# Two thirds of the w_out conversion beside the first layer instead of the attention, with a new order table, another queue for one pair and fewer warm-up products

## The chip, the cores and the metric

One core of one Trainium2 chip. The metric is the device time of one execution in microseconds, lower is better; the figure for the kernel before is the median of three runs. The engines of the core run side by side, each its own instructions in order: TensorE (PE, matrix products; PEld are its weight loads), VectorE (DVE), ScalarE (ACT), GpSimd (POOL) and SyncE (SP). SP, ACT and POOL also issue transfers (DMA) between the chip's memory (DRAM) and the core's, each on a queue of its own. Products come out in PSUM, which has 8 banks.

## The reference, cut to what matters

```python
def _attn_ref(q, k, v):                       # batch 4, 12 heads, 448 positions, 64 wide
    scores = scale * np.matmul(q, k.transpose(0, 1, 3, 2)) - np.log(S)
    attn = 1.0 / (1.0 + np.exp(-scores))      # a sigmoid, not a softmax
    return np.matmul(attn, v).astype(np.float32)

def _moe_ref(x, w_gate, w_val, w_out, rms_g): # 1792 tokens, 768 wide, 1536 inside
    rms = np.sqrt(np.mean(x * x, axis=-1, keepdims=True) + 1e-06)
    xn = x / rms * rms_g
    g = xn @ w_gate
    silu = g * (1.0 / (1.0 + np.exp(-g)))
    val = xn @ w_val
    return (silu * val @ w_out).astype(np.float32)

def _moe2_ref(x, w_in, w_out):                # 2048 inside
    h = x @ w_in
    g = h - np.tanh(h)
    return (g @ w_out).astype(np.float32)
```

The output is `_moe2_ref(_moe_ref(_attn_ref(q, k, v)))`, the heads laid side by side. q, k and v come in 32-bit floats, the weights of both layers in 64-bit floats.

## The kernel before

**Stages.** First the attention, two heads (a pair) at a time, 6 pairs for each of the 4 batches. Then the first layer: products with w_gate and w_val (called Ag and Av; phase A) and with w_out (phase B). Then the second: w_in (C) and w_out2 (D). Each layer is done for batches 0 and 1 first (BATCHES[0]), then for 2 and 3.

**Products.** A 32-bit factor is split into a high and a low part that TensorE multiplies fast, and three products (high-high, high-low, low-high) stand for one. On top of that, matrices are taken as 2 by 2 blocks and multiplied with seven block products instead of eight, from sums such as S1 to S4 of the weights' blocks A11 to A22 and T1 to T4 of the activations'. So for each weight VectorE and ACT make values, sums and parts. `values32` (L510) makes a 32-bit value out of a raw 64-bit tile `raw`: a cast into the tile `zero` (by ACT or VectorE, L438 in the profile, the line of a helper) and one VectorE instruction at L510. `total` (L574) makes a sum. `split` (L521) makes the two parts. There are 2 buffers for `raw`, one tile `zero` for all, and at most 3 buffers `cv` for values and sums.

**Jobs.** The first layer's first half is a list of jobs 0 to 14: five pair jobs (Ag, Av, Ag, Av, Ag; 21 products of three each), a job of phase B with set 0 of w_out (42 of three), four pair jobs, set 1, three pair jobs, set 2 (used plain, with the four blocks alone). Each job makes the factors of the job two ahead (`conv`) and loads the raw tiles of the one four ahead (`load`).

**w_out.** Its blocks come in three sets. `rows_early` makes a set's units: load the raw tiles by POOL's queue, convert, sum, and store the values in DRAM, again by POOL, as `wB`. Set 0 and 1 have four blocks and, less one, the four sums, 7 stores; set 2 has four stores. Jobs 5, 10 and 14 load them again. In the kernel before all three sets' units, with casts by VectorE (`by_dve`), are spread over the attention of batches 0 to 2 (`rows_b`, `ROWS_B`). The second layer's w_out2 (D), four sets, goes the same way beside the first layer's second half.

**q, k and v.** `pair_load` loads a pair: q and k by SP's queue, but 128 columns of the very first k by ACT's, v of batches 0 and 1 by POOL's. From the third pair on q and k are split as well (`split_qk`, L732).

**The order.** The code adds each piece of work with its reads, writes and buffers to a plan; `lay` then gives it out. Among the pieces that can start soon it takes the one of lowest rank in `ORDER`, a table of one number for every piece, written out as text. So the order of instructions on each engine, and with it the order of the queues, is the table's, within what the buffers' caps allow. The program issues them with semaphores, and an engine that waits holds all behind it.

**Warm-up.** `N_WARM` products of zeros (L446) run on TensorE while the first q and k come in.

Of the kernel before, what the change touches and what calls it, by code (L numbers as in the profile page):

```python
# [244 lines left out]
2zn2ZU5fM7Lu9LSBC672y4ss0WM24q3fM0n70DR5fq0IM1G233P3oh48l3l61M_1do2Cr89Q96_0uM16r2S522A3HH1yx3Ou3Pf29E2f34LM2Do37L2k52Cr
2_y3fn48I3B61Oe4Pg2xM0kg3iv4fn3h42Gn14W3CM2cp3Zw3wM45d41K4BD4AF4QI2GK2u62h_1wT41k4J61gB2g94vR4vM1J43Tf3sS4aY1-l56T1-M12j
3hI0dw1Hx1pZ2FZ3ky3gy2Iy1oi1rH2tX1JA5912Mt2lT2r13G80xf02v3Z_37B0S43IB1rE0R32vN5Ae49D4p-3BP6184MVNGI5NB3hZ8ZS1ri1M94P_2i0
2o_33O3sX32b29L18k1Py1Kf3Vz2Ux2PE3he0_l3Bv2OB2u81l034i2o92Xj3P22Au2AU2mq1n91uv07m0mV2Gx1Rx24y2pH0zp1cc0QE2m63lw1KL33Y0n1
2J34dY2x22fg11V14E2845Lx12n3mr3RK3D35PL3Wv4qC4Oy6DU2hU5KQ4-92Sc3Fh0tO4Db3uN1Va4SY3fT3Sz2uz3e51Ox1nS3Na2nW5M37oH2_Y3ky2Lz
2YU35b1vK3u83FE2B22l33Nz63u4ZS56n3lO2hT4S_5gk3-d5P25IR5U943P0i45TW5r97OX5Eh3Pq3XA2YK5dv0gg4et2pX7pi0QV4Gz3ek4Cs3IC2Hu5b9  # L250
4zu5KT4TC4Rp1Ry1oL4nH37734N3fh2iy4nD3oi5tk3dh4Ob7aV4a44wb0X-73K0473l464X3hg3lA4Hj2gY3TT3j93fe2rb7dP4l95fy4pU5gu33g49S5Hg
4PC7fg3Ro44b58A02W5iV5mg4_R50j3x64aH4SI6qg38b5nU49DAG44OU3yV6RP7Ab6iJBwR5mz12p2nm4rH39r4HS5fq96I4W84FD76r1390Xa3Qk0Rh03Q
8Do42w5HrH4y7MZ43J4HF6qn39p47i5wJ4FF87_3x72cc2s50Jr0D43130s70m-1JE4Gs0GWH1V7MD3DbEyb2lE4ke7eg73Q8aF77IE0202-4OO6zz7y05Eu
0h06ME63l54u4IZ6PTBAv02-5vZ71w4wlAxB9GX38kABw9my0GY7lA7Wr3NZ3rF9tN3SF7pO69PAUP5A05ZG2ll3oQ57F4ay2rw8WQ2wW0001PkAIr3870kT
5LC5CIDOS0Wt0Yo4p368E6ni0VC5kA9vd4QIIY_0NQJwm0TM7UBAb2EalG2n64g51w6yp5WV6ip6bp6T8A8s3ed1qF4ma2IU1157Cc4Rz1C28W0BeP7-y6as
8Tw5h76W-0M04gw7YO8cECVP6XW8pN5BH7pk2G92bJ6kc7Le7aM0aD1O0A898DQ0go7dABk444L0wU5r18O83xP5Qr0J63tfDjl1pD81HByz7PQ3349qK6Sk
1R9BtyE6UB18CdFFuMDtH0cO9NY6wv19EBL13i4IHv6bJBJOElH8tX76e9M9DSfBxmGch6Rw5BDBxw3zh1y5BsU7Yp7g67gJ2a002-EMV7TM3If4xG7a800r
9YI1wL9oC5pP04TKFB5iGB4a0PA8ie0VD0d0FecAJrBY79pfFdDCAo5h4B10DHp0BuHbOK3y9UjAVxCFo5NDD48EwUNPHD1YFcsHhpDBrIZmERY16X0TQGN8
EyvD-qE3A6Lt0Z90EDGcwDV50YV0Dv0BtEVBEDe9EZ0CKGn3Cta4ao0pSCvq0D_000LGuAdI9nZ81WAcC8n62nUElp38pATI7bqM2DA0h8Nj6B3FVE1asPdV
6oUGOW4djEOZPqvNZ1NKMHyoC6TC-xBEfCLs9Dp7ZABW794g4QuDKjDCBCoMCIuBn0ARDBh0DnmFRa87x2a41OI1QC05f05gKLoEqWHotGQe6BsINu8t_8PI  # L260
MT70XMMx28aV6gGAyFKpwDkE43O1_85ko220McH1DM1ug6ncKj997d5X87gOJjf0WfOcA8L_7xmATvLur79b96QNQ2PHt0aPHSEOq9UikIxMIahJAnPM9LlP
AuNJ7ZEeLIMCFABJQvGFxEhr9vp6uZ6-bFoq7m38FgDIn9AN6zi7gzE7o7ih7Qv7GM6br5Z08Ei63qEND6ts7Q55NO9vn5lu6Aj9C791L6Pa7a36sk6vY8UU
6z05uz9OT8-NCSFBmn1Cn7xz6ua6aG7bM5u87NI7FA4fC7TD9rT82Q6pn4xg7-AARL3NTAE46Fn7cs8aJ6Yy6xm6hd8R29PU6-S8L257u5sb6Fa7Kf7AM6bE
5E55K08DM6Z_5jR8aD3Lo7oo67U6iG6ZE6bh7LA6Zc6zP7vi6Rn5pf7ew7aZ6rc83E7PC76p7JF8nN6Gw8z97rO78w4_s6li6GJ6FY63U59Y5DP2YH3Jy2_g
8xY61w6Vy3Cg6x-5ti5Pt49L68C7iL6Hw4Ch6zW7YM7Au4zQ3TT4TH3oQ8WP5Tw7k73Lm7M26Zl6yH7sW7AH5sk5Tk7kA7io7lb7Ra7035RW9pA8f40G02oX
6bM7fl8tW6dd79571T6oe7oc8B_7MH5E157B3uS4_x9OL4_o3sR7gE69w7kH8dX75U7Ol53N2y_3bH6dd6AA2P872_5Ek8076oX3NO6mG5_q55g7s16Fa61n
5fb8Aa81_7xB7Au87C3-T6jj7tQ7oL2z59g883U8Yv3Do7qO7a79Bm74l9022gT8MW8Sh51R1Lv5mp7yV7bW73a7AZ7w86Zl9RX4aq4lh5Jh8SG9So6V075V
87f8q65wD7_08Fs6yJ8Dc8ZUA0W7jq8Dk75-7Iy8QZ75Z7n18628SI8oS8EF6rI4pr76X88G6NU7b56-V4hm8Rn7628QD8THBps8y492Y6yX7lr7wv8yC6g2
6jO8IaAAe8QW7gz7SbAJV5pQ97u7d_9e_8ce7nk5sQ6eC8U77Qs87O8ry8b16oN7O58dB6bO7Lj73F7UP85s8eR7eTAAQ8pK7O87r79DT7xc90tAIQ87SA-v
# [1125 lines left out]
```

## Time and profile before

| | us |
|---|---|
| median of 3 runs (1032.61 to 1040.37) | 1033.85 |
| the profiled execution | 1032.65 |
| its span, first to last instruction | 1030.8 |
| TensorE busy | 1015.3 (98%) |
| VectorE busy | 790.4 (77%) |
| ACT busy | 676.7 (66%) |
| POOL busy | 155.8 (15%) |

Busy times overlap, and a busy TensorE need not be at its pace, since its products are pipelined and their ends modelled: how many it sends in a stretch tells more. Times in rows are us from the span's start. The attention is from the start to about 140 us, the first layer's first half from there to about 380 us, its second half to about 620 us, the second layer from there to the end.

### The profile page before, as it was taken

The page shows a single profiled execution, that of the slowest core. Times are in us where ns is not written, and L with a number is a line of the kernel's source. Part 1 is how long each engine was busy: PE and PEld are TensorE (multiplying, and loading weights), DVE is VectorE, ACT ScalarE, POOL GpSimd, SP SyncE. Part 2 cuts the span into 40 slices and gives each one's busy share as a digit, 9 for nine tenths or more (in the row PEclk, how much of TensorE's full clock was granted, in tenths as well). Part 3 has the DMA queues.
Part 4 walks back from the last instruction along what each step waited for, and adds up shares of the span by engine and source line. Part 5 has one row for each costly group of instructions (what it writes and reads, how often), then busy time and mean ns, then how long its engine had stood idle before and what let it go on. Part 6 is the DMA issues. An engine that isn't in the chain of part 4 may idle for free.

```text
span 1030.8 us, 15321 instructions
## 1 busy us (share of the span) xinstructions
PE 1015.3 (98%) x5261; PEld 876.4 (85%) x5261; DVE 790.4 (77%) x1281; ACT 676.7 (66%) x1235; POOL 155.8 (15%) x217
## 2 busy tenths in 40 slices
...
GB/s 312 285 338 309 234 235 235 298 189 305 197 195 327 141 259 319 361 265 355 214 128 242 219 199 266 99 311 254 235 159 252 264 188 94 225 129 197 121 228 135
DMA packets 101997, 240.03 MB, mean 233 GB/s; under 512 B 11456, under 2 KB 59520, under 8 KB 101920
## 3 DMA queue, kind: packets, MB, share of 16 engines
...
q8 instruction: 41, 0.67, 0.3%
...
HBM read 149.36 MB, written 89.66 MB: 232 GB/s over the span
## 4 chain that ended last, share of the span: by engine, by line
PE 69%; issue 13%; DMA 10%; DVE 3%; POOL 3%; ACT 1%; SPq 0%; POOLq 0%; DVEq 0%; ACTq 0%
PE ps L1135 37%; PE ps L1080 21%; PE ps L1160 6%; PE ps L813 3%; DMA part<-in_qkt 2%; DMA wD<-part 2%; PE ps L756 2%; POOL out L958 2%; DMA out<-unit 1%; DMA part<-wAg 1%; DMA part<-wB 1%; DMA raw<-in_w_out 1%; DMA wB<-part 1%; DVE part L521 1%; PE ps L777 0%
## 5 line engine op out<-in xcount | busy, mean ns | idle before, releaser
L1135 PE MATMUL ps<-unit,part 128*128 128x448 f32 x2520 | 521.0, 365 | 8.4 <-DVE unit L1016 4.6
L1135 PEld LDWEIGHTS ps<-unit,part 128*128 128x128 f32 x2520 | 470.9, 187 | 52.4 <-DVE unit L1016 6.3
L1080 PE MATMUL ps<-unit,part 128*128 128x448 f32 x1512 | 311.4, 364 | 0.0
L1080 PEld LDWEIGHTS ps<-unit,part 128*128 128x128 f32 x1512 | 283.5, 187 | 22.3
L521 DVE TENSOR_TENSOR part<-part 128x768 fp32r<-128x768 f32 (+1 forms) x244 | 215.4, 891 | 76.8 <-ACT part L438 55.0
L438 ACT COPY unit<-ps 128x448 f32<-128x448 f32 x291 | 150.3, 536 | 127.1 <-PE ps L1135 46.5
L438 ACT CAST part<-part 128x768 fp32r<-128x768 f32 (+1 forms) x236 | 183.1, 786 | 41.1 <-DMA wD<-part 8.0
L887 DVE TENSOR_TENSOR unit<-unit 128x448 fp32r<-128x448 f32 x252 | 152.1, 620 | 35.2 <-ACT unit L438 27.1
L438 ACT CAST unit<-unit 128x448 fp32r<-128x448 f32 x262 | 143.3, 570 | 39.3 <-DVE unit L999 17.9
L1016 DVE TENSOR_TENSOR unit<-ps,unit 128x448 f32<-128x448 f32 x168 | 103.9, 622 | 48.0 <-PE ps L1135 19.1
L765 ACT ACTIVATE unit<-ps 128x448 f32<-128x448 f32 x168 | 80.3, 565 | 27.6 <-PE ps L756 15.3
L892 DVE TENSOR_TENSOR unit<-unit 128x448 f32<-128x448 f32 x144 | 86.4, 619 | 14.4 <-DMA unit<-sumB 7.9
L958 POOL DMA_DIRECT2D sumB<-unit x48 | 41.8, 946 | 273.2 <-DVE unit L1016 168.8
L510 DVE SCALAR_TENSOR_TENSOR part<-raw,zero 128x768 uint32<-128x768 uint32 x68 | 64.8, 953 | 6.4 <-ACT zero L438 5.9
L438 ACT CAST zero<-raw 128x768 f16<-128x768 bf16 x52 | 56.0, 1078 | 16.5 <-DMA raw<-in_w_out 6.5
L813 PE MATMUL ps<-unit,part 128*64 128x448 f32 x288 | 59.4, 548 | 0.0
L1160 PE MATMUL ps<-unit,part 128*128 128x448 f32 x288 | 59.2, 364 | 0.0
L958 POOL DMA_DIRECT2D out<-unit x36 | 31.1, 1055 | 175.3 <-DVE unit L1016 161.7
L1160 PEld LDWEIGHTS ps<-unit,part 128*128 128x128 f32 x288 | 54.0, 187 | 4.2
L756 PEld LDWEIGHTS ps<-unit 64*128 64x128 f32 x396 | 35.6, 184 | 17.7 <-ACT unit L765 9.8
L756 PE MATMUL ps<-unit 64*128 64x448 f32 x396 | 47.3, 375 | 0.5 <-DVE unit L732 0.5
L813 PEld LDWEIGHTS ps<-unit,part 128*64 128x64 f32 x288 | 18.5, 136 | 30.5 <-issue 23.8
...
## 6 DMA issues: line engine op xcount, KB each, us to landing
raw<-in_w_out POOLq DMA_DIRECT2D x28, 768.0 KB, 7.9
part<-wD SPq DMA_DIRECT2D x56, 384.0 KB, 6.8
part<-wB SPq DMA_DIRECT2D x36, 384.0 KB, 5.5
raw<-in_w_in SPq DMA_DIRECT2D x16, 768.0 KB, 5.1
wC<-part SPq DMA_DIRECT2D x30, 384.0 KB, 3.3
part<-wC SPq DMA_DIRECT2D x30, 384.0 KB, 3.9
...
wD<-part POOLq DMA_DIRECT2D x28, 384.0 KB, 7.0
```

What stands on the lines that cost most here:

```text
L438: add(engines, lambda e: (nc.scalar.copy if e == "ACT" else nc.vector.tensor_copy)(to(), of()), reads, writes)
L521: add({**dve(n, psum=False), **pool(n)}, lambda e: ENG[e].tensor_sub(lo(), of(), hi().bitcast(F32)), [*reads, *kh], [*kl])
L756: nc.tensor.matmul(ps[i].tile[:, :S], lhsT=k_of(w, b, c, i), rhs=x.tile[rows, :S], start=q == 0, stop=q == len(terms) - 1)
L765: add(act(S, psum=True), lambda e: nc.scalar.activation(to.tile, ps.tile[:, :S], AF.Sigmoid, bias=-math.log(S), scale=1.0 / math.sqrt(D)), ...
L813: nc.tensor.matmul(ps.tile[HEADS[i], :S], lhsT=v_of(v, b, c, i), rhs=a[c][i].tile, start=opens and c == 0, stop=not opens and c == MAIN - ...
L887: add({**pool(S), **dve(S, psum=False)}, lambda e: ENG[e].tensor_sub(t["l"].tile, of.tile, t["h"].tile.bitcast(F32)), [of["t"], kh], [kl])
L892: add({**dve(S, psum=False), **pool(S)}, lambda e: ENG[e].tensor_sub(t.tile, x.tile, y.tile), [x["t"], y["t"]], [t["t"]])
L958: add(queue("POOL", True), lambda e: nc.gpsimd.dma_start(out=d.tile, in_=t.tile, accum_op=ALU.add), [t["t"], d["t"]], [d["t"]], moved=move ...
L1016: add(dve(S), lambda e: nc.vector.tensor_add(t.tile, ps.tile[:, :S], t.tile), [ps["t"], t["t"]], [t["t"]])
L1080: nc.tensor.matmul(ps.tile[:, :S], lhsT=part(a), rhs=x[b].tile, start=n in (1, 5) and kp == 0 and q == 0, stop=kp == n_kp - 1 and q == 2, ...
L1135: nc.tensor.matmul(ps.tile[:, :S], lhsT=part(a), rhs=x[b].tile, start=n in ((1, 2, 5) if opening else (1, 5)) and i == 0 and q == 0, stop= ...
L1160: nc.tensor.matmul(ps.tile[:, :S], lhsT=wt, rhs=a[p].tile, start=start and i == 0, stop=stop and i == 2, skip_group_check=True)
```

## The change

Five things. `N_WARM` goes from 9 to 7. The cap of `cv` goes from 3 to 5 buffers, in the same room of 20. q and k of the second pair (batch 0, pair 1) are issued by ACT instead of SP. The units of sets 1 and 2 of w_out are no longer in `rows_b`; they are added beside the first layer's jobs 2, 3, 4 (set 1) and 6, 7, 8 (set 2), where ACT makes the casts. And every number of the table `ORDER` is new, so that all engines' order is new.

```diff
-N_WARM = 9
+N_WARM = 7
+ROWS_AT = {1: 2, 2: 6}
...
-        "part": (N_PART, {"cv": 3, "again": 4, "vs": 6, "qkr": 9, "whl": 8, "op": 10}),
+        "part": (N_PART, {"cv": 5, "again": 4, "vs": 6, "qkr": 9, "whl": 8, "op": 10}),
...
-        part("SP", lambda: tq.tile, both[:, :S], tq[0], 4 * S)
+        first = "ACT" if (b, p) == (0, 1) else "SP"
+        part(first, lambda: tq.tile, both[:, :S], tq[0], 4 * S)
...
-            part("ACT" if hi == P else "SP", lambda lo=lo, hi=hi: tk.tile[:, lo:hi], both[:, S + lo:S + hi], tk[n], 4 * (hi - lo))
+            part("ACT" if hi == P else first, lambda lo=lo, hi=hi: tk.tile[:, lo:hi], both[:, S + lo:S + hi], tk[n], 4 * (hi - lo))
...
-    rows_b = by_dve([u for i in range(n_sets("B")) for u in rows_early("B", i)])
+    rows_b = by_dve([u for i in range(n_sets("B") - len(ROWS_AT)) for u in rows_early("B", i)])
...
+    rows_late = {}
+    for i, at in ROWS_AT.items():
+        rows = rows_early("B", i)
+        rows_late.update({at: rows[:1], at + 1: rows[1:5], at + 2: rows[5:]})
...
-        ahead = conv(j + AHEAD) + [lambda: load(j + 2 * AHEAD)]
+        ahead = conv(j + AHEAD) + rows_late.get(j, []) + [lambda: load(j + 2 * AHEAD)]
```

What the table makes of it, at three places. Lines of the changed kernel are one or two higher: L438 is L439 there, L510 is L511, L732 is L734, L756 is L758, L777 is L779, L797 is L799, L813 is L815, L849 is L851.

VectorE at the opening, the kernel before from its fourth instruction on (`part` is q or k, `unit` a part of it, `raw` a tile of w_out):

```order
L438 CAST unit<-part 128x448
L732 TENSOR_TENSOR unit<-part,unit 128x448
L438 CAST zero<-raw 128x768
L438 CAST unit<-part 128x384
L510 SCALAR_TENSOR_TENSOR part<-raw,zero 128x768
L732 TENSOR_TENSOR unit<-part,unit 128x384
```

The same place of the changed kernel:

```order
L439 CAST unit<-part 128x448
L734 TENSOR_TENSOR unit<-part,unit 128x448
L734 TENSOR_TENSOR unit<-part,unit 128x384
L439 CAST unit<-part 128x448
L734 TENSOR_TENSOR unit<-part,unit 128x448
L439 CAST unit<-part 128x384
```

The raw tile of w_out has gone from between the splits of the third pair, and POOL's loads of w_out stand behind the v of six pairs.

TensorE around the norm of batch 1 (L849), the kernel before (L756 are scores, L777 and L797 the pairs' last positions, L813 products with v):

```order
L797 MATMUL ps<-unit,part 64x448 x4
L756 MATMUL ps<-unit 128x448 x18
L813 MATMUL ps<-unit,part 64x448 x6
L756 MATMUL ps<-unit 128x448 x18
L813 MATMUL ps<-unit,part 64x448 x6
L777 MATMUL ps<-part 64x448 x4
L797 MATMUL ps<-unit,part 64x448 x4
L849 MATMUL ps<-ones,unit 128x1 x3
```

The same of the changed kernel, from the same L799 on:

```order
L799 MATMUL ps<-unit,part 64x448 x4
L758 MATMUL ps<-unit 128x448 x18
L815 MATMUL ps<-unit,part 64x448 x6
L758 MATMUL ps<-unit 128x448 x12
L851 MATMUL ps<-ones,unit 128x1 x3
```

The norm has moved forward by 6 products of scores, 6 of v and the tail.

ACT beside job 8 of the first layer, the kernel before (with buffer numbers; `raw_3455` is a tile of w_gate):

```order
L438 CAST part_3521<-part_3496 128x768
L438 CAST zero_80<-raw_3455 128x768
L438 COPY unit_3540<-ps_3478 128x448
L438 COPY unit_3548<-ps_3485 128x448
L438 COPY unit_3554<-ps_3492 128x448
```

The changed kernel (`raw_3218`, `raw_3298` and `raw_3349` are tiles of w_out):

```order
L439 CAST zero_80<-raw_3218 128x768
L439 CAST part_3325<-part_3161 128x768
L439 COPY ps_3335<-ps_3310 128x448
L439 CAST part_3342<-part_3205 128x384
L439 CAST zero_80<-raw_3298 128x768
L439 COPY unit_3365<-ps_3345 128x448
L439 CAST part_3371<-part_3148 128x768
L439 COPY unit_3386<-ps_3310 128x448
L998 ACTIVATE unit_3401<-ps_3335 128x448
L439 CAST unit_3408<-unit_2831 128x448
L439 CAST zero_80<-raw_3349 128x768
```

Three casts of w_out tiles now stand among the copies out of PSUM (`ps`) of this job.

## Rows read from the trace of the kernel before

**Rows 1.** The page, part 1: TensorE's busy time, share of the span, instructions
```profile
PE 1015.3 (98%) x5261; PEld 876.4 (85%) x5261; DVE 790.4 (77%) x1281; ACT 676.7 (66%) x1235; POOL 155.8 (15%) x217
```

**Rows 2.** Chain of waits: start us, us, what; one pair of heads, then a layer
```profile
28.11 2.02 PE ps L756 x18
30.13 2.41 PE ps L813 x12
...
209.31 21.84 PE ps L1080 x108
```

**Rows 3.** Timeline of TensorE, the opening: start, us, instruction, count, idle before
```profile
1.16 3.54 PE L446 MATMUL ps<-mark 128*128 128x448 bf16 x9 [1.16 <-DVE mark L442]
...
9.00 2.53 PE L756 MATMUL ps<-part 64*128 64x448 f32 x12 [0.82 <-DMA part<-in_qkt]
...
14.77 0.67 PE L756 MATMUL ps<-unit 64*128 64x448 f32 x4
15.90 1.29 PE L756 MATMUL ps<-unit 64*128 64x448 f32 x10 [0.46 <-DVE unit L732]
```

**Rows 4.** Timeline of TensorE, the norm of batch 1
```profile
88.59 1.01 PE L849 MATMUL ps<-ones,unit 128*128 128x1 f32 x8 [0.89 <-DVE ps L852]
```

**Rows 5.** Timeline of TensorE, start of the first layer
```profile
142.79 9.03 PE L1135 MATMUL ps<-unit,part 128*128 128x448 f32 x41
152.70 4.15 PE L1135 MATMUL ps<-unit,part 128*128 128x448 f32 x18 [0.88 <-DVE part L521]
157.52 2.69 PE L1135 MATMUL ps<-unit,part 128*128 128x448 f32 x12 [0.66 <-DVE part L521]
```

**Rows 6.** Timeline of TensorE, four later stops
```profile
339.31 2.89 PE L1135 MATMUL ps<-unit,part 128*128 128x448 f32 x13 [0.78 <-ACT ps L438]
...
477.27 3.90 PE L1135 MATMUL ps<-unit,part 128*128 128x448 f32 x18 [0.69 <-ACT unit L438]
...
510.01 2.30 PE L1135 MATMUL ps<-unit,part 128*128 128x448 f32 x10 [2.33 <-DVE unit L1016]
...
797.26 2.09 PE L1135 MATMUL ps<-unit,part 128*128 128x448 f32 x9 [1.60 <-DVE unit L1016]
```

**Rows 7.** Stretches: us, busy PE, PEld, DVE, ACT, POOL, PEclk, DMA share, GB/s
```profile
15.00:140.00 125.00, 123.56 (x883) 62.31 (x881) 98.87 (x187) 98.39 (x216) 26.38 (x42) 1.00 0.83 291
140.00:160.00 20.00, 18.38 (x87) 15.25 (x84) 18.40 (x33) 12.23 (x22) 0.00 (x0) 1.00 0.53 185
160.00:206.00 46.00, 46.00 (x233) 42.69 (x232) 41.40 (x71) 31.62 (x51) 3.04 (x2) 1.00 0.82 283
206.00:285.00 79.00, 79.00 (x393) 73.23 (x392) 65.56 (x103) 50.22 (x87) 0.00 (x0) 1.00 0.68 232
```

**Rows 8.** Groups by line: count | busy us, mean ns | idle before, releasers
```profile
L510 DVE SCALAR_TENSOR_TENSOR part<-raw,zero 128x768 uint32<-128x768 uint32 x14 | 13.4, 957 | 0.5 <-DMA wB<-part 0.3
L438 DVE CAST zero<-raw 128x768 f16<-128x768 bf16 x15 | 9.2, 611 | 11.6 <-DMA raw<-in_w_out 11.6
L574 DVE TENSOR_TENSOR part<-part 128x768 f32<-128x768 f32 x8 | 7.6, 955 | 0.9 <-DMA wB<-part 0.9
...
L438 ACT CAST zero<-raw 128x768 f16<-128x768 bf16 x21 | 22.6, 1077 | 6.4 <-DVE part L510 3.2 <-DMA raw<-in_w_val 2.1 <-DMA raw<-in_w_gate 1.1
```

**Rows 9.** Transfers of the first 8 us, then of the first 140 us
```profile
DMA packets 1093, 1.80 MB, mean 226 GB/s; under 512 B 141, under 2 KB 782, under 8 KB 1093
...
DMA packets 17949, 41.07 MB, mean 293 GB/s; under 512 B 2352, under 2 KB 12400, under 8 KB 17936
```

**Rows 10.** Issues up to 140 us, then 140 to 350: KB, median us to landing
```profile
raw<-in_w_out POOLq DMA_DIRECT2D x12, 768.0 KB, 8.0
wB<-part POOLq DMA_DIRECT2D x18, 384.0 KB, 6.1
...
raw<-in_w_gate SPq DMA_DIRECT2D x10, 768.0 KB, 6.2
```

**Rows 11.** Waits from 440 to 512 us: who for whom, us, times, longest
```profile
ACT part L438 <- DMA wD<-part: 8.0, 3, 3.3
```

More of the change, by code (lines that the diff above doesn't have):

```diff
@@ L245 @@
[L245 to L269, printed above, removed]
@@ new lines @@
+0nJ0P30291bG0_H0PD1680000Y31cF05f0eV12b4yI2kY0ZS1cJ0XU0l81Xg0bA0J_00l1k500e0290fe0921PE05F0PQ1EP0u31Ki02w05o0e80Hd0UX02w
+2kp0XA1r_2Ml2In05z08o0S30D70mu1FP0FG1Re1jE0kt05316s0DN1zo0zr1sY0cF1Zy0U60cg0Ur0530x30NY0530o_1Y90000-N2qe0AR1zH2VP0QN08-
+3Rk10z1kF1Qw3560OV03h0Pl0Ql3Br0We1Nn1e51kT4cG1jE11i4Ke0ZL0zm3g50WY0qB1PK0G62SV1U51p503p1102Ff0lo2se0-C0JA1Hn1-v2gE1q_029
+10j2Dd48z22n0ej1Nh2et21W1IW2dY2x51L439J3lP1RP29r3uf2sj2G13sB3h-4UZ4pG4gr4YK5SG5QG2gl46H34N1kR3a76AN2pQ1q01CD2I431L3OX5LA
+3aP4Sy5QA52E5275fL4UK5BV4R44Yy6Ey2yz3VM5VK4ox3a65GY3d847z6RV6q26Ii6ZJ5el5fP44G6Mc3ty7KD8K05cz5LR60Q4bG5dl5ub7yN5bd3z35P4
@@ new lines @@
+3f_5ps3Ca4x05QX7rG3OT65T4nF6LC3CC3ax3fQ6XF6o-5nk6n-4fQ6jk6XH3jI5Vr3zR2_m2V257q2lr8e-5Ke4Rl6ZX2mD53549d4PV3mi5N46bW5Zo1Q3
+1kL06P3FT2Eq5yA5JN6VF5K37iW8Qv4955jr50-0aB0l_0tA44B4MV2iv3B_0001Ib3WM5OS5Zo8dt2q00741SH06b65l63-2XN4V92MU39r0iR4lt5Dh6jy
+3jI32n6k46nc1LkIlR97n3Ps69z54F4QL3zS5hh5rr7PW6bnBPCA2N2Pj5hs7mg2em3Ga6M06Ti4736S765_ELB7rj06S8Vm5Q45uH2f10005c94q262341o
+1-Z6Mz8CJ6Ol4sn5mY5MP6uQ1Nn5cJB617FP8PE9v05Ge4ti8w2CPx6ei2Nk93n5iZ6py6325Vm51-8Mf06x5VF5t06tY5UM2vqA6F7YA0i266v5ZD5GvAB1
+56_5FK3PP1aU2wA4kC1CY1md2dx3qG7XV8nN4RW9fq4oU6nm6vc3fb7DdEueB6v6H02o05br6gl6oY5z86lM80Q0hg16q5BA0az1G455b1Ts0ot34x5Qf304
@@ new lines @@
+3Tq5PU4t75U45-E4BJ4zl2RW02TBu12x11DW5CY0wa03Y5Rj2dc8oM06v0YrAWj0002AQ05cGnk2r1BA5000IAf1T42QQ0cg0sG5Sr3II1Z19xj0m4HsvGT2
+BlgBU23I0Gq5J-_KuSB2MAGw02H0mCHhW0XTKTwECtJ1jL8IAd0EAxG138tK8deBBf8WWGsuCFKAX59VE5iI6yJ7XxAow6ss9DH7P16rsBGZ9xh6CK7QN7D8
+5za7d07Gj8eL77K4ncBXEG4HFdcEY9AuY6KQ49n8uW8X87zD7rh8zM6U_4Vg8MF6HG0_09nm9DR9GD9fl9f37IU9cA5uX6I88dXA15AYw7EaBcyBnt7UM686
+Cmd9mF9uB9fZ92Z3wJ0neBfmAJl4tN5v74cU6N08cM8gx7TT98-9Q672q6IA86X3Sn2_ZBWx9ug8he96p8A44cu4S768T6dJ5cv5MpA-Y9Uo5qg3jj9gx6X8
+98P4jE8v2091NrOBDk9Xl81W6qs5I05Px5K379C5IU4_j5m15944n-8SI74y62J6zj65V63I6Sc9PuBMF6yh5ke7ou8T47jZ6BeA1N7am5UQ9ql5ZQ3TY7Dz
```

200 lines of the change are left out of this document (105 added, 95 removed).

## The prediction

> **What bounds the kernel now.** I read the totals first. TensorE is busy for 1015.3 us of the span [rows 1], so this is a TensorE kernel, and the reader should ask only where it does not send products at its own pace. The chain of waits gives that pace [rows 2]: a pair of heads of the attention is 2.02 us of scores and 2.41 us of products with v, with nothing between them, and 108 products of a layer take 21.84 us, 0.2022 each. Then TensorE's timeline shows its stops. There are four kinds, in order of time: the opening, where it waits 0.82 us for the second pair's q and k at 9.00 and 0.46 us at 15.90 for VectorE [rows 3]; a norm of 0.89 us at 88.59 [rows 4]; the start of the first layer at 152.70 and 157.52 [rows 5]; and later stops at 339.31, 477.27, 510.01 and 797.26, together 0.78 + 0.69 + 2.33 + 1.60 = 5.4 us [rows 6]. The stretches show why the third kind exists: from 140 to 160 VectorE is busy for 18.40 of 20 us, while in 15 to 140 it is at 98.87 of 125 with 0.83 of the transfer engines' time taken [rows 7]. So the attention itself is not bound by the conversions; what they cost is VectorE's debt at its end. All w_out conversions lie ahead of that end.
>
> **The change, part by part.**
> *Leaving the attention.* Sets 1 and 2 are 8 loads, 8 conversions, 4 sums (set 2, used plain, has none) and 11 stores. On VectorE that is 8 x 0.611 (casts) + 8 x 0.957 + 4 x 0.955 = 16.4 us [rows 8]. TensorE's stops at 152.70 and 157.52 wait for it: from 142.79 to 157.52, in 14.73 us, it sends 41 + 18 = 59 products [rows 5], which at 0.2022 are 11.9, so 2.8 us are lost. I take all of it as gained, since 16.4 us less work is some six times the loss and VectorE has little rest in that stretch to use up; the other end is no gain, if what is late there is an operand and not VectorE.
> *The norm at 88.59.* It waits for a memset of VectorE's that stands behind splits and sums. In the new order the norm stands 12 products of scores after the attention's L815 group instead of after the whole next turn, so it is sooner wanted, but VectorE has fewer raw tiles ahead of it. I take the 0.89 us as gained; the other end is 0.
> *The opening.* VectorE's new first rows hold no raw tile, and POOL loads v of six pairs before the first w_out. So L732, for which TensorE waits at 15.90, is ready in time. TensorE's work from 9.00 runs to 14.77 + 0.45 without a stop, and the four products at 14.77 cover 1.13 us up to 15.90 instead of 0.45, so 0.7 us are to be gained. The second pair's q and k go by ACT's queue, where they stand behind a table load, while the third pair's take their place on SP's. If the queues share the engines evenly, the third pair's 480 KB (224 of q, 256 of k), which used to come behind the second's, now come in beside them: 0.48 MB at the 226 GB/s of the first 8 us is 2.1 us, at the 293 of the first 140 us 1.6 us [rows 9]. Then TensorE stops longer at 9.00, but not again at 15.90. Between -0.7 and 2.1 - 0.7 = +1.4 us; I take -0.3, since POOL's 768 KB tiles, which came in beside the first pairs, are gone from there.
> *Two products of zeros less* (N_WARM says 9 to 7; the seven that are left are what the change names). TensorE reaches the first scores 2 x 0.39 us earlier (nine zeros take 3.54 us [rows 3]), and then waits for the second pair at 9.00 all the same: 0.
> *Coming back beside the first layer.* VectorE gets 8 x 0.957 + 4 x 0.955 = 11.5 us, ACT the casts, 8 x 1.077 = 8.6 us [rows 8]. VectorE rests 46.00 - 41.40 = 4.6 us from 160 to 206 and 79.00 - 65.56 = 13.4 us from 206 to 285, ACT 14.4 and 28.8 [rows 7]. Set 1 needs 7.6 us of VectorE in about the first stretch, more than the 4.6; the 16.4 us that it owes less cover the rest. Without that cover it would be 3.0 us. Then there is the wait for loads: ACT takes its instructions in order, and behind a raw tile's cast stand copies out of PSUM for which TensorE's banks wait. POOL's loads of a raw tile take 8.0 us to land against 6.2 of SP's [rows 10], and there are two raw tiles for all. The nearest rows are those of w_out2, 16 loads of the same kind beside the same layer's second half, where TensorE's stops of [rows 6] at 477.27 and 510.01 are 3.0 us: 0.19 a load, 1.5 us for 8. Between 0 and that, with a new rest at hand, I take 0.8.
> *The new table elsewhere.* No edit is aimed at the later stops; the table is new there as well, so the 5.4 us may shrink or grow: 0, plus or minus 3.
> *Sum:* -2.8 - 0.9 - 0.3 + 0.8 = -3.2 us, from the profiled execution's 1032.65 us (span 1030.8) to 1029.4. The median of the three runs, 1033.85, is 1.2 us above the profiled one, the lowest 1032.61; I keep to 1029.4.
>
> A rule of the Trainium skill speaks against the new queue: "DMA: Bandwidth & Descriptors", section "Issuing engines are not separate DMA queues", has all transfers interleave on the same 16 engines, so that starting them from several engines saves the issue alone. No row shows two of these queues loaded with pairs at once, so the trace neither bears it out nor denies it; by the rule the opening is the +1.4 above and the sum 1031.1.
>
> **The rivals.**
> *The opening loses what the rest gains a part of.* The second pair is late by 1.6 to 2.1 us, as worked out above. For it: both queues wanted the same engines, whose share is 0.83 up to 140 [rows 7]. Against it: POOL's 768 KB tiles are no longer among the first transfers. Time: 1032.65 - 2.8 - 0.9 + 0.8 + 1.4 = 1031.1. By the rule cited above this is the case that comes.
> *No gain.* TensorE's stop at 152.70 is for a factor (L521) that needs its own raw tile, loaded and cast before it. If that load is late, VectorE's freed time is idle time and the 2.8 us stay. For it: VectorE has 11.6 us of waits for w_out tiles before their casts [rows 8], so a load can rule its order. Against it: 10.6 MB less to move (8 x 0.79 + 11 x 0.39) in the first 140 us, of 41.07 [rows 9]. Time: 1032.65 - 0.9 - 0.3 + 0.8 = 1032.2.
> *Slower.* The loads beside the first layer come late where ACT's casts stand, ACT holds the copies behind them, and TensorE's banks stay full. Price: if each of the four groups of two loads stops TensorE as at 510.01, for 2.33 us [rows 6], that is 9.3 us instead of 0.8: 1032.65 - 4.0 + 9.3 = 1038.0. For it: in the w_out2 stretch ACT waited 8.0 us for stores of the same kind [rows 11]. Against it: there all four sets of w_out2 go through beside the operands of a whole layer. It decides from 4.0 us / 4 = 1.0 us a group.
> *Deeper.* The new table takes the later stops away too: 1029.4 - 5.4 = 1024.0.
>
> **How the numbers follow.** Forecast 0.42; opening late 0.20; no gain 0.14; slower 0.14; deeper 0.10. The forecast, 1029.4, is that of the likeliest. From 1023.5 to 1037.5 the range holds all cases but half of the slower and a part of the deeper one, about 0.13 in all with the spread of the later stops. The likeliest case alone would be 1027 to 1032. A measurement of this kernel tells about 1% from no change, which is 10.3 us: under 1023.5 or over 1044.2 from the median. Faster by more needs the deeper case and the opening's best end: 0.06. Slower by more needs the slower case at over one and a half times its price: 0.05. Within 1%: 0.89.
>
> **What would show it.** Right: no stop of TensorE over 0.3 us between 140 and 160, VectorE with rest there; no raw tile ahead of L734 in VectorE's opening and a first split product near 15; the norm's idle time gone; in 160 to 285 VectorE at over 90% without a stop of TensorE. Wrong: the idle row before the second pair's scores grows from 0.82 to over 2; rows of ACT's cast of a raw tile waiting for in_w_out for over 2 us at a time with a TensorE stop behind them between 165 and 285; or the stops at 477 to 510 and 797 move by more than 3 us together, which nothing in this sum foresees.

## The result and the profile after

The changed kernel takes 1045.85 us (median of 6 runs, 1043.81 to 1049.95) against 1033.77 for the kernel before (6 runs): ratio 1.0114, interval 1.0087 to 1.0141. It is slower by a little over 1%, outside the range of the prediction (1023.5 to 1037.5). The profiled execution (1047.32 us) has a span of 1045.5 us, 14.7 more than that of before. It is one of the longer of the six: by the medians 12.1 us were lost, and by the traces that follow 14.7.

The page after, totals [rows 1], and the granted clock in 40 slices:

```profile
PE 1021.9 (98%) x5259; PEld 881.9 (84%) x5259; DVE 788.1 (75%) x1278; ACT 681.0 (65%) x1238; POOL 153.5 (15%) x217
...
PEclk9999999999899999999999999999999999999999
```

TensorE's work is the same but for two products of zeros, and yet it is busy for 6.6 us more: some of its products ran at a lower clock, as the short stretches further down show. Its timeline shows where. Columns are start, us, instruction, count, idle time before and what ended it. The opening, to set against [rows 3]:

```profile
3.88 4.05 PE L758 MATMUL ps<-part 64*128 64x448 f32 x12
10.33 4.22 PE L758 MATMUL ps<-part 64*128 64x448 f32 x12 [2.40 <-DMA part<-in_qkt]
...
17.80 2.09 PE L758 MATMUL ps<-unit 64*128 64x448 f32 x18
```

The second pair's scores begin at 10.33 instead of 9.00 and take 4.22 us instead of 2.53; the stop at 15.90 is gone, as foreseen. The norm of batch 1 no longer waits [rows 4], but that of batch 2 does. And the start of the first layer has no stop left [rows 5]:

```profile
85.30 1.03 PE L851 MATMUL ps<-ones,unit 128*128 128x1 f32 x8
...
119.53 1.03 PE L851 MATMUL ps<-ones,unit 128*128 128x1 f32 x8 [0.65 <-DVE ps L854]
...
146.52 11.18 PE L1137 MATMUL ps<-unit,part 128*128 128x448 f32 x54
157.54 0.93 PE L851 MATMUL ps<-ones,unit 128*128 128x1 f32 x8
158.40 13.81 PE L1137 MATMUL ps<-unit,part 128*128 128x448 f32 x67
```

The stretches that answer to [rows 7] (us, busy time of PE, PEld, DVE, ACT, POOL, then granted clock, DMA share, GB/s): VectorE is freer up to 160, and the transfer share is lower in the attention and higher from 206 on, 0.84 for 0.68.

```profile
15.00:140.00 125.00, 124.35 (x885) 63.79 (x878) 90.17 (x177) 97.84 (x217) 14.88 (x25) 1.00 0.63 215
140.00:160.00 20.00, 20.00 (x108) 15.00 (x107) 17.66 (x34) 12.51 (x22) 1.91 (x2) 1.00 0.66 208
...
206.00:285.00 79.00, 75.97 (x362) 69.87 (x362) 61.98 (x95) 49.08 (x82) 7.03 (x13) 0.96 0.84 304
```

Then come stops that the kernel before did not have, and the later ones stand elsewhere than in [rows 6]:

```profile
273.92 11.36 PE L1137 MATMUL ps<-unit,part 128*128 128x448 f32 x41 [3.03 <-DVE unit L1018]
...
345.11 7.19 PE L1137 MATMUL ps<-unit,part 128*128 128x448 f32 x27 [4.42 <-DVE unit L1018]
...
756.29 1.89 PE L1137 MATMUL ps<-unit,part 128*128 128x448 f32 x8 [2.70 <-DVE unit L1018]
...
804.98 5.48 PE L1137 MATMUL ps<-unit,part 128*128 128x448 f32 x18 [2.27 <-ACT unit L439]
```

The 41 products from 273.92 take 11.36 us; at 0.2022 they are 8.3. The clock accounts for it, as short stretches show (columns as above):

```profile
273.00:277.00 4.00, 3.08 (x8) 2.78 (x9) 4.00 (x7) 2.74 (x5) 1.33 (x3) 0.53 0.75 190
345.00:348.00 3.00, 2.89 (x8) 2.59 (x9) 2.83 (x6) 2.79 (x5) 0.00 (x0) 0.50 0.99 352
756.00:760.00 4.00, 3.71 (x18) 3.45 (x19) 4.00 (x8) 3.60 (x7) 0.00 (x0) 1.00 0.28 93
805.00:809.00 4.00, 4.00 (x12) 3.59 (x13) 3.69 (x8) 1.75 (x5) 0.19 (x1) 0.59 1.07 293
```

After the stops of 3.03, 4.42 and 2.27 us the granted clock is 0.53, 0.50 and 0.59 in these stretches: TensorE runs mostly at half, 1.2 GHz of 2.4. After that of 2.70 it is 1.00.

**Where the time lies.** Both kernels send the same products, so I take, for a given product, its start less the work sent ahead of it at its own pace (0.2022 us each in the layers, likewise for scores, products with v and norms; the products of zeros are not counted as work). Only differences between columns mean something. This is worked out from the starts in the traces:

| up to | before | after | grown by, before | after | difference |
|---|---|---|---|---|---|
| scores 200 (62 to 64 us) | 9.40 | 11.74 | | | +2.3 |
| L1135/L1137 product 40 (148 to 150) | 12.16 | 14.50 | 2.76 | 2.76 | 0.0 |
| product 200 (184) | 14.80 | 14.51 | 2.64 | 0.01 | -2.6 |
| product 800 (387 to 398) | 16.14 | 27.06 | 1.34 | 12.55 | +11.2 |
| the end | 24.64 | 39.38 | 8.50 | 12.32 | +3.8 |

The sum is +14.7, the difference of the spans. The first row is partly the execution's: of the six executions traced with this opening (the changed kernel's, experiments 3, 5, 6 and 7, and the first try of 9), two are 2.3 us behind the kernel before at score 200, and four are 0.4 to 0.7 us ahead of it. The row from 200 to 800 is steadier: 12.6 us in experiment 1 and 14.1 in experiment 7, which leave that stretch as it is.

**At 270.** VectorE waits 5.62 us for a store, until 267.63, and ACT and TensorE behind it; the store took 10.9 us to land. Timeline of SP's queue, then of VectorE, then transfers issued from 240 to 275 us (KB each, median us to landing):

```profile
256.65 0.32 SPq L589 DMA_DIRECT2D wAv<-part  x1
```

```profile
267.63 0.96 DVE L522 TENSOR_TENSOR part<-part 128x768 fp32r<-128x768 f32 x1 [5.62 <-DMA wAv<-part]
```

```profile
raw<-in_w_out POOLq DMA_DIRECT2D x3, 768.0 KB, 7.5
...
wAv<-part SPq DMA_DIRECT2D x3, 384.0 KB, 10.9
```

POOL issues loads of set 2 at 255.62 and 259.56, around that store. The split waits because it is to be written where the stored tile lies.

**At 340.** ACT waits 6.38 us, again for a store, which SP had sent at 328.46:

```profile
340.36 1.56 ACT L439 CAST part<-part 128x768 fp32r<-128x768 f32 x2 [6.38 <-DMA wAg<-part]
```

Its value was ready near 322.8 (VectorE's sum); three reloads of x stand ahead of it on SP's queue. Why SP sends so late can be read from SP's own waits (315 to 332 us: for whom, us, times, longest):

```profile
SPq L589 <- DMA raw<-in_w_val: 2.7, 1, 2.7
```

In this program, as the semaphores in the trace show, the transfers of SP use eight of them in turn, so one goes out only when the one eight places ahead of it has landed. This store is the eighth behind the raw load of 314.14, which landed at 328.09; the reload at 325.10 waited in the same way for a store that landed at 325.02. So a transfer that lands slowly holds what stands eight places behind it.

The pair that is converted here is the first half's last. Its raw tiles are loaded (issued) at 310.55 and 314.14; in the kernel before at 288.49 and 303.70. POOL issues twelve stores `sumB` at 305.8 to 318.9, the sums of the phase B job, which add to what lies in DRAM.

### The profile page after: what moved, and what is told of

It reads as the page before. It is cut to its first block, busy times and chain, and to the rows that moved or that the text cites. A ratio compares the mean times of both kernels' runs of the same rounds, so it can differ in the third digit from the quotient of the medians.

```text
span 1045.5 us, 15338 instructions
## 1 busy us (share of the span) xinstructions
PE 1021.9 (98%) x5259; PEld 881.9 (84%) x5259; DVE 788.1 (75%) x1278; ACT 681.0 (65%) x1238; POOL 153.5 (15%) x217
## 4 chain that ended last, share of the span: by engine, by line
PE 50%; DMA 3%; issue 1%; DVE 1%; POOL 0%; ACT 0%; DVEq 0%; SPq 0%; ACTq 0%; POOLq 0%
PE ps L1137 25%; PE ps L1082 23%; PE ps L1162 3%; DMA wC<-part 1%; DMA sumB<-unit 1%; DMA out<-unit 1%; DMA raw<-in_w_in 1%; DVE unit L1018 0%; POOL out L960 0%; DVE part L522 0%; ACT unit L439 0%; DVE unit L1001 0%; DVE unit L1006 0%; DVE unit L889 0%; DVE part L607 0%
## 5 line engine op out<-in xcount | busy, mean ns | idle before, releaser
L1137 PE MATMUL ps<-unit,part 128*128 128x448 f32 x2520 | 526.3, 367 | 15.7 <-DVE unit L1018 11.5
L1137 PEld LDWEIGHTS ps<-unit,part 128*128 128x128 f32 x2520 | 476.0, 189 | 60.3 <-DVE unit L1018 13.3
L439 ACT COPY unit<-ps 128x448 f32<-128x448 f32 x291 | 150.5, 536 | 113.0 <-PE ps L1137 42.3
L439 ACT CAST part<-part 128x768 fp32r<-128x768 f32 (+1 forms) x236 | 182.3, 787 | 45.9 <-DVE part L607 9.3
L439 ACT CAST unit<-unit 128x448 fp32r<-128x448 f32 x261 | 145.0, 571 | 45.9 <-DVE unit L1001 23.6
L511 DVE SCALAR_TENSOR_TENSOR part<-raw,zero 128x768 uint32<-128x768 uint32 x68 | 64.8, 953 | 28.8 <-ACT zero L439 18.5
L439 ACT CAST zero<-raw 128x768 f16<-128x768 bf16 x60 | 64.7, 1078 | 17.2 <-DMA raw<-in_w_out 8.4
L815 PE MATMUL ps<-unit,part 128*64 128x448 f32 x288 | 59.5, 547 | 0.0
L758 PEld LDWEIGHTS ps<-unit 64*128 64x128 f32 x396 | 35.4, 184 | 18.2 <-ACT unit L767 9.3
L758 PE MATMUL ps<-unit 64*128 64x448 f32 x396 | 47.5, 376 | 0.0
L607 DVE TENSOR_TENSOR part<-part 128x384 f32<-128x384 f32 x80 | 43.3, 553 | 1.0 <-DMA wAv<-part 0.6
```

Source lines behind the costliest of these rows:

```text
L439: add(engines, lambda e: (nc.scalar.copy if e == "ACT" else nc.vector.tensor_copy)(to(), of()), reads, writes)
L511: add(dve(NW, psum=False), lambda e: nc.vector.scalar_tensor_tensor(out=c.tile.bitcast(U32), in0=r.tile[:, :NW, 1], scalar=13, in1=z.tile, ...
L758: nc.tensor.matmul(ps[i].tile[:, :S], lhsT=k_of(w, b, c, i), rhs=x.tile[rows, :S], start=q == 0, stop=q == len(terms) - 1)
L1137: nc.tensor.matmul(ps.tile[:, :S], lhsT=part(a), rhs=x[b].tile, start=n in ((1, 2, 5) if opening else (1, 5)) and i == 0 and q == 0, stop= ...
```

## The experiments

Each group of runs was measured beside the kernel before on one chip. Its median there was 1033.1 to 1033.8 us, so runs of different groups are best compared by their ratios to it. The account of a run is that of its profiled execution alone. Where an experiment keeps the changed kernel's own order, the table `ORDER` holds that order itself, so that only the edit differs:

```diff
-        for n, e in self.lay([ORDER_UNIT * n for n in numbers(ORDER)]):
+        for n, e in [(n >> 3, self.ENGINES[n & 7]) for n in numbers(ORDER)]:
```

The same account as above, for the main runs (us; a column less one to its left is what is lost in between; the last time is the median):

| kernel | scores 24 | product 400 (250 us) | 600 | 800 | 1700 | end | median, ratio to before |
|---|---|---|---|---|---|---|---|
| before | 8.4 | 14.8 | 14.8 | 16.1 | 21.3 | 24.6 | 1033.8 |
| after | 11.4 | 14.5 | 20.6 | 27.1 | 30.1 | 39.4 | 1045.9, 1.0114 |
| second pair by SP | 7.5 | 10.6 | 15.7 | 23.2 | 25.5 | 36.5 | 1042.5, 1.0089 |
| sets 1 and 2 left out | 11.4 | 14.5 | 14.5 | 23.3 | 25.4 | 35.0 | 1040.6, 1.0059 |
| set 2's loads by SP | 8.6 | 11.6 | 11.7 | 20.5 | 23.1 | 34.5 | 1041.8, 1.0079 |
| without the 12 sums | 8.7 | 11.7 | 15.7 | 16.0 | 17.4 | 23.5 | 1036.1, 1.0025 |
| second layer's old order | 8.4 | 11.6 | 17.6 | 25.6 | 28.3 | 31.9 | 1041.1, 1.0077 |
| before, second pair by ACT | 9.7 | 14.4 | 14.5 | 15.6 | 21.1 | 25.5 | 1034.9, 1.0017 |
| three repairs | 8.0 | 11.0 | 11.0 | 20.3 | 23.0 | 30.6 | 1035.7, 1.0022 |
| five repairs | 7.6 | 10.7 | 11.1 | 13.7 | 15.9 | 21.5 | 1030.4, 0.9966 |

**1. The second pair back on SP.**

```diff
-        first = "ACT" if (b, p) == (0, 1) else "SP"
+        first = "SP"
```

> The changed kernel with its order written out piece by piece, and one thing undone: q and k of the second pair are issued by SP, behind the first pair's, as before. Theory 1 (ACT's queue makes the second pair late): TensorE's stop before the second pair's scores goes from 2.40 us to about 0.8, the granted clock there is full, and some 2.3 us of the time go, 1045.85 to about 1043.5. Rival (the third pair's and v's transfers make it late on any queue): the stop stays over 2 us and the time within 0.5 us. The stops at 270.5 and 340.3 stay under either.

Measured: 1042.51 us, ratio 1.0089 (1.0055 to 1.0123). TensorE's opening:

```profile
4.07 2.71 PE L758 MATMUL ps<-part 64*128 64x448 f32 x12
8.11 2.53 PE L758 MATMUL ps<-part 64*128 64x448 f32 x12 [1.33 <-DMA part<-in_qkt]
```

The second pair comes at 8.11 instead of 10.33, the clock is full, and 3.9 us fewer are lost up to product 400 (10.6 for 14.5). The intervals of the two ratios overlap. How much is the queue's: on ACT's the second pair came at 10.33 here, and in the six other runs with it at 8.96 to 10.46; on SP's in six runs of the changed opening or its like at 7.89 to 8.55. So it costs 0.4 to 2.6 us by itself, and where the stop is followed by half clock, 1.7 us more (4.22 for 2.53). That happened in two of the six executions with the changed opening and ACT's queue; the table shows the other kind in experiments 5, 6 and 7, which lose 11.6 or 11.7 up to product 400, only 1 us more than with SP. The pair is not issued later on ACT (1.66 and 2.05 us there, 1.65 and 2.12 on SP); what changes is that the third pair goes out beside it, at 1.65 and 2.12 instead of 2.59 and 3.07. The Trainium skill, "DMA: Bandwidth & Descriptors", section "Issuing engines are not separate DMA queues", says that transfers from all issuing engines interleave on the same 16; the trace agrees, since a queue of its own brought the pair later and not sooner.

**2. The same edit on the kernel before.**

```diff
-        part("SP", lambda: tq.tile, both[:, :S], tq[0], 4 * S)
+        part("ACT" if (b, p) == (0, 1) else "SP", lambda: tq.tile, both[:, :S], tq[0], 4 * S)
```

(k likewise.)

> The kernel before in its own order with one change: q and k of the second pair are issued by ACT, behind its part of the first k. Theory 1: TensorE's stop before the second pair's scores grows from 0.82 to over 2 us, and the kernel loses 2 to 4 us, 1033.4 to about 1036.5. Rival: with POOL's w_out tiles among the first transfers the second pair is late on either queue, and the time stays within 1 us.

Measured: 1034.87 us, ratio 1.0017 (1.0001 to 1.0033). The stop grows from 0.82 to 2.95 us, as expected, but the pair starts only 1.25 us later, at 10.25, and by product 400 nothing of it is left (14.4 for 14.8), since later waits of before take it up. The profiled execution ends 0.8 us later, and the median of 10 runs is 1.7 us above that of before: less than the 2 to 4 expected, more than the rival's 1. No half clock followed this stop of 2.95 us. What a late pair costs depends on the waits behind it.

**3. Sets 1 and 2 left out.** The 39 pieces are not issued, and jobs 10 and 14 read set 0:

```diff
-            w = again(whole_w[ph, i], ROWS.index(n))
+            w = again(whole_w[ph, 0 if ph == "B" else i], ROWS.index("A22" if (ph, n) == ("B", "A21") else n))
```

> The changed kernel in its own order, but the loads, conversions, sums and stores of w_out's sets 1 and 2 are left out; jobs 10 and 14 load set 0's rows instead (what is left out is part of the computation). Theory 1 (these pieces beside the first layer cause the stops at 270.5 and 340.3): both stops go, TensorE's loss from 250 to 400 us falls from 12.5 us to under 2, the time from 1045.85 to about 1034.5. Rival 2 (the new table causes them whatever is converted there): a loss of over 6 us stays in that stretch, the time is over 1040.

Measured: 1040.56 us (1036.0 to 1043.2), ratio 1.0059. By its numbers this is rival 2 (8.8 us lost from product 600 to 800, over 1040); by its places it is half a hit: nothing is lost at 270 (61 products from 263.82 on without a stop), but the stop near 340 stays and is longer:

```profile
341.30 8.89 PE L1137 MATMUL ps<-unit,part 128*128 128x448 f32 x35 [6.74 <-DVE unit L1018]
```

So the two stops have different causes. The one at 270 is that of the moved pieces; the one at 340 is in the order that is left when they are gone. In that order the last pair's raw tiles are loaded at 304.41 and 308.00, as late against TensorE's work as in the changed kernel, though the eight tiles of sets 1 and 2 take no `raw` buffer any more.

**4. The move without the new table, and the table without the move.** The move alone has before's rank for every piece that is not moved; the table alone has the new rank for each. (The other edits of the move are those of the change.)

```diff
+                if held[k] + x > (3 if k == "cv" and oldest > CV_LATE else cap[k]):
-ORDER = (the new numbers)
+ORDER = (the old number of each piece; a moved one has that of the TensorE piece it stands behind)
```

> The kernel before with the move alone: sets 1 and 2 of w_out are converted beside jobs 2 to 4 and 6 to 8 by ACT's casts, with cv at 5 up to there and 3 from the first layer's second half on; all other pieces keep their rank of the table before; nine products of zeros, SP's queue. Theory 1: the stops at 152 and 157 go (-2.8 us), stops of 5 to 11 us together appear between 165 and 390, the time is 1036 to 1042. Rival 2 (the table): 1030 to 1033, no stop over 1.5 us there.

Measured: 1056.33 us, ratio 1.0212. Worse than the changed kernel, and than expected: it loses 5.5 us from product 40 to 100, where the stops of 151 to 157 were to go, and 25.5 from product 200 to 800, 8.1 of them at once near 337. The last pair's raw tiles are loaded at 318.8 and 323.4.

```diff
-ORDER = (the old numbers)
+ORDER = (the new number of each piece, on the kernel before)
```

> The kernel before with the ranks of the new table alone: sets 1 and 2 stay in the attention (each of their pieces with the rank of the TensorE piece that it stood behind), cv at 3, nine products of zeros, SP's queue. Theory 1: no stop over 1.5 us between 250 and 350; the later stops are those of the changed kernel (705, 753, 798, 802), so that the time is 3 to 5 us over before, 1036 to 1039. Rival 2 (the table is the cause of the stops at 270 and 340 as well): over 1042.

Measured: 1065.74 us, ratio 1.0314. This expectation missed by far: by product 40 it is already 15 us behind the kernel before (norms wait 2.23 and 4.37 us), presumably because the ranks leave no place for sets 1 and 2 in the attention. From product 200 to 800 it loses only 2.4 us, without a stop near 340; the last pair's raw tiles are loaded at 301.3 and 304.6. So a table fits one placement, and the two halves cannot be costed one by one. What the two show together is the lateness of the last pair. Taken against TensorE's work (each time less the kernel's excess over before at product 600), the last two raw tiles are loaded 16 and 5 us later than before in the changed kernel, 15 and 5 later with the move alone, and 3 and 15 sooner with the table alone; the stop near 340 comes in the first two. So the new ranks do not make the lateness by themselves, and the move makes it under either table. By which way is not shown. It is not that tiles of w_out hold the buffers while the kernel runs, since experiment 3 keeps the lateness without these eight tiles; it lies in the order that `lay` gave out with them. The two `raw` buffers, which they share there with the layer's tiles, are a likely reason. A third buffer wasn't tried.

**5. Set 2's first two loads by SP, each behind a store.**

```diff
-                rs[x] = load_raw(SECOND[ph][4 * i + FOUR.index(x)], ROWS_BY[ph])
+                rs[x] = load_raw(SECOND[ph][4 * i + FOUR.index(x)], "SP" if (ph, i) == ("B", 2) and x[1] == "2" else ROWS_BY[ph])
```

> The changed kernel in its own order, but the first two loads of set 2 (768 KB each, issued by POOL at 255.62 and 259.56) are issued by SP, each right behind the store that SP issues there. Theory 1a (the loads compete for the transfer engines with SP's store of wAv, which took 10.9 us to land and for whose buffer VectorE waited 5.62 us): the store lands in under 8 us, TensorE's stop of 3.03 us at 270.5 and the half clock behind it go, the time falls by 4 to 6 us to about 1041. Rival 1b (what is late there is the work of ACT and VectorE for set 2): the stop stays over 2 us, the time within 1.5 us of 1045.85.

Measured: 1041.82 us, ratio 1.0079 (1.0058 to 1.0100). TensorE goes through the place without a stop, VectorE's wait for the store falls to 1.36 us, and the stores wAv issued from 240 to 275 take 7.6 us instead of 10.9:

```profile
257.75 17.55 PE L1137 MATMUL ps<-unit,part 128*128 128x448 f32 x86
```

```profile
260.50 0.96 DVE L522 TENSOR_TENSOR part<-part 128x768 fp32r<-128x768 f32 x1 [1.36 <-DMA wAv<-part]
```

```profile
wAv<-part SPq DMA_DIRECT2D x3, 384.0 KB, 7.6
```

The same work by ACT and VectorE, the same bytes, issued at nearly the same place of TensorE's work (253.32 and 256.89, with TensorE 2.9 us earlier); only their queue and place behind the stores differ. 1a holds. All 6.1 us lost there are won, but part is given back at the next stop (8.8 us from product 600 to 800 for 6.5). The same page of the Trainium skill, section "Queues, rings and completion order", says that each transfer engine takes turns, packet by packet, between the queues that have work; a store on one queue then shares its engines with big loads on another. The trace agrees: on one queue behind the store the loads no longer delayed it.

**6. Without the twelve accumulating stores.** The pieces are not issued (the sum of the second set is left out of the result). In the order as written out:

```diff
-POOL: sumB<-unit, twelve (305.80 to 318.9)
```

> The changed kernel in its own order without the twelve accumulating stores sumB (224 KB each) that POOL issues at 305.8 to 318.9; the sum of the second set is thereby left out of the result. Theory 3a (the last pair's raw loads at 310.5 and 314.1 and its stores fall into the transfers of these twelve): the load of 314.1 is cast by 323 instead of 328.5, TensorE's stop of 4.42 us at 340.3 falls below 1.5, the time by 4 to 6 us to about 1041. Rival 3b (the pair's conversions stand too late in the order whatever the transfers do): the stop stays over 3 us.

Measured: 1036.06 us (1031.4 to 1040.1), ratio 1.0025: about 9 us gained, where 4 to 6 were expected. The stop is gone, and nearly nothing is lost from product 600 to 800 (0.3 us for 6.5). The other gains of its account are not explained; its profiled execution is the shortest of the ten; the stretch of 305 to 325 us without them, then in the changed kernel:

```profile
305.00:325.00 20.00, 20.00 (x101) 18.54 (x100) 12.72 (x20) 11.72 (x19) 0.54 (x1) 1.00 0.88 309
```

```profile
305.00:325.00 20.00, 20.00 (x101) 18.54 (x100) 13.19 (x20) 12.51 (x22) 11.04 (x13) 1.00 1.00 207
```

With them the transfer engines are busy all the time and move 207 GB/s, without them 309 at a share of 0.88. One detail missed: the raw tile is still cast 14.3 us after its load is issued (309.27 to 323.60), because its cast stands behind a copy of ACT's that waits for TensorE. But the load itself lands 5.0 us after its issue, for 14.0 in the changed kernel, and the stores wAg issued from 305 to 345 take 6.2 us (median) for 10.0. So the twelve delay both, and the late load does its harm on SP's queue: the store eight places behind it now goes out at 316.70, and ACT no longer waits for it.

**7. The second layer in the old order.** Ranks of before for the pieces from number 2600 on (after some 550 us); otherwise the changed kernel.

```diff
-ORDER = (the new numbers)
+ORDER = (the new numbers up to piece 2600, the old ones behind it)
```

> The changed kernel up to about 550 us; from there on the order is that of the kernel before (its ranks for the pieces of the second layer, cv at 3 there). Theory 4 (in the second layer the new table alone costs): the stops at 705, 753, 798 and 802 give way to those of before at 785 and 797, and of the 9.3 us lost there some 6 go: 1040. Rival: what is late in the second layer comes from the first, and the loss stays over 8 us.

Measured: 1041.10 us, ratio 1.0077 (1.0060 to 1.0094). From product 1700 to the end 3.6 us are lost instead of 9.3, against 3.4 in the kernel before. The stops of 2.70 at 756 and 2.27 at 805 are gone. So these lie in the order of the new table there; the first layer, with its stops, is the same in both. How much the order is worth varies with the execution: behind product 1700 the old order loses 3.4 to 7.6 us in the rows of the table, the new one 6.1 to 11.4.

**8. Three repairs together**: edits 1, 5 and 7.

> Three repairs together on the changed kernel: second pair's q and k by SP, the first two loads of set 2 by SP behind the stores, the second layer in the order of the kernel before. If the three causes are separate, their gains add: -1 to -4 at the opening, nothing lost at 270, 7.6 us at 331 as in the run with SP's loads, 3.3 in the second layer: 1033 to 1036. If they are not, over 1038.

Measured: 1035.68 us (12 runs), ratio 1.0022 (1.0006 to 1.0038). The gains add up: alone the three edits lower the ratio by 0.0025, 0.0035 and 0.0037, together by 0.0092. The account does so less well: in the profiled execution, the longest of the twelve, 9.3 us are lost from product 600 to 800 and 7.6 behind 1700, for the 7.6 and 3.3 expected. Left is the stop at 331 to 340:

```profile
337.82 7.35 PE L1137 MATMUL ps<-unit,part 128*128 128x448 f32 x25 [6.70 <-DVE unit L1018]
```

**9. The store that ACT waits for.** A first try on the changed kernel moved the store:

> The changed kernel in its own order, with one store moved: SP issues the store wAg that ACT's cast waits for until 340.36 ahead of the three reloads of x (321.37, 321.96, 325.1) instead of behind them. Theory 3c (SP, held by the slow raw load of 314.1, sends this store too late): SP issues it by 323.5 instead of 328.46, it lands by 335, the stop of 4.42 us at 340.3 falls to about 1, the time by 3 to 5 us. Rival 3d (it lands late because the engines are full, whenever it is issued): the stop stays over 3 us.

Measured: 1054.32 us, but the edit put the store ahead of the sum that fills its tile, so that VectorE waited 16.46 us for it: it says nothing on the question. Nor does a run of the three repairs with the same misplaced store and the edit of experiment 10, where VectorE waited 14.69 us: 1043.46 us, where 1027 to 1030 was expected and 1032 to 1036 by the rival. The next moves the three reloads of x behind the store instead, on top of the three repairs (SP's order as written out):

```diff
 SP: wAv<-part
-SP: unit<-x, three
 SP: wAg<-part
+SP: unit<-x, three
```

> The three repairs (second pair by SP, set 2's first two loads by SP, the second layer in the old order) and a fourth: the three reloads of x that SP issues at 311.5, 311.9 and 314.9 in the run of the three repairs stand behind the store wAg of 317.98 instead of ahead of it. Theory 3c (SP, held by the slow raw load, sends this store too late): the store goes out by 313.5, lands by 326, the stop of 6.9 us at 331 falls to about 2, the time from 1035.7 to about 1031. Rival 3d (it is late because the engines are full, whenever it is issued): the stop stays over 5 us, the time within 1.5 us.

Measured: 1032.70 us, ratio 0.9982 (0.9965 to 0.9999). SP sends the store at 313.55 instead of 317.98, and the stop is halved:

```profile
333.92 6.40 PE L1137 MATMUL ps<-unit,part 128*128 128x448 f32 x17 [3.36 <-DVE unit L1018]
```

In the run of the three repairs it went out when the raw load eight places ahead of it had landed, at 317.92; now the transfer eight places ahead is a store that lands at 311.72. ACT still waits 5.10 us for it, until 328.95, so it takes 15 us to land: between 3c and 3d. Its place on SP's queue counts, and so does the load on the transfer engines.

**10. The load of w_out2 behind the reloads, on SP.**

```diff
-                rs[x] = load_raw(SECOND[ph][4 * i + FOUR.index(x)], "SP" if (ph, i) == ("B", 2) and x[1] == "2" else ROWS_BY[ph])
+                rs[x] = load_raw(SECOND[ph][4 * i + FOUR.index(x)], "SP" if (ph, i, x[1]) == ("B", 2, "2") or (ph, i, x) == ("D", 0, "A21") else ROWS_BY[ph])
```

> The same four repairs and a fifth: the first load of w_out2 (768 KB, POOL, 312.25 in the run of the three repairs, 16.6 us to land) is issued by SP behind the reloads of x. Under 3c and 3a together the stop at 331 goes below 1.5 us and the time to 1027 to 1030, under the kernel before. Under 3d with 3a (the engines are full, and each transfer taken out of that stretch helps) this run gains over 2 us on the one before it. If what fills the engines are the twelve accumulating stores alone, it gains under 1 us.

Measured: 1030.43 us (1028.88 to 1033.49, 7 runs), ratio 0.9966 (0.9950 to 0.9981): 0.3% under the kernel before.

```profile
333.20 7.14 PE L1137 MATMUL ps<-unit,part 128*128 128x448 f32 x34 [2.04 <-DVE unit L1018]
```

2.3 us better than the run before it, as 3d with 3a has it, though the two intervals overlap. The load goes out on another queue and some 10 us later as well (322.78), and which of the two helps isn't separated. The stop is down to 2.04, not under 1.5; ACT no longer waits for the store, but for VectorE's sum (3.63 us until 328.08).

## Why the prediction was wrong, step by step

- **What bounds the kernel** was right: by the account, all of the difference is time in which TensorE stands or runs at half clock.
- **Leaving the attention, -2.8**: -2.6 measured. The stops of [rows 5] are gone and VectorE has rest in 140 to 160 (2.3 of 20 us for 1.6). The *no gain* rival falls.
- **The norm, -0.9**: gone where it stood, but the norm of batch 2 now stops TensorE for 0.65 us, and from score 200 to the layer's product 40 the account grows by 2.76 in both kernels; together 0. I looked only at the norm that waited.
- **The opening, -0.3**: +2.3. The rival *opening loses* was right in its mechanism, engines shared by two queues. Its +1.4 was too small because the stop was priced as idle time alone: the pair was 1.3 us late for 1.6 to 2.1, the 0.7 at 15.90 was gained, and in this execution half clock added 1.7 us, a term that the sum did not have. Four of six executions with this opening lack that half clock and stand 0.4 to 0.7 us ahead of the kernel before, so there -0.3 was about right. The table load, ahead of the pair on ACT, delayed nothing (experiment 1). The listed sign, an idle row of over 2 us before the second pair, came (2.40). No run isolates the two products of zeros.
- **Conversions beside the layer, +0.8**: +11.2. This is the step that failed. I took the price from stops in the w_out2 stretch, 0.19 us a load, and looked for casts waiting for their raw tiles. They hardly wait: 1.8 us in all for in_w_out from 165 to 290. What the moved work does is delay others: its loads delay a store of the layer on SP (experiment 5: 6.1 us with the clock), and the order that it forces has the layer's own last pair loaded later, so that this pair meets the twelve accumulating stores (experiments 4 and 6: 6.5 us from product 600 to 800, where before loses 1.3). The first is shown by an edit that takes it away. For the second, that the twelve stores are needed for the stop and that the move makes the pair late are shown; why `lay` puts it so late is not. The *slower* rival had nearly the right size, 9.3, by luck: its reason was a cast held by its own load. Its own [rows 11], ACT waiting for stores, were nearer to what came. So I gave it 0.14, and the casts waiting over 2 us at a time that I listed as a sign never came; what I listed for being right there, VectorE at over 90% without a stop, did not come either (61.98 of 79 us from 206 to 285, and a stop of 3.03). The row that could have told was [rows 7]: a transfer share of 0.82 in 160 to 206 and 0.68 in 206 to 285, before 10.6 MB were added. I read it for VectorE's rest alone.
- **The new table elsewhere, 0 plus or minus 3**: +3.8, just outside; from product 800 to 1700, where the stops at 477 to 510 lie [rows 6], 2.2 us less are lost, and behind 1700 5.9 more, which the old order there mostly gives back (experiment 7).

Of the 17.9 us between the forecast's -3.2 and the account's +14.7, the failed step holds 10.4, the table 3.8, the opening 2.6, the norm 0.9 and leaving the attention 0.2. Slower by over 1% had a chance of 0.05.
